# Values of two batches cast while loading on the GpSimd DMA queue, and a first batch that begins with 512 tokens

## Chip, core and metric

The kernel runs on one core of a Trainium2 chip. The metric is the device time of one execution in microseconds (us), lower is better. Every time below is a median of at least four runs, and each ratio is against runs of the kernel before on the same chip. The experiments were spread over three chips; the kernel before took 226.0 to 226.5 us in every set, so medians of different sets may be compared to about half a microsecond. A profile shows one execution; its span is some 1.7 us shorter than the time of the run it comes from.

Names: TensorE is the matrix engine (PE), VectorE is DVE, ScalarE is ACT, GpSimd is POOL, SyncE is SP. Loads are issued on two queues, that of SyncE (a plain copy) and that of GpSimd (whose loads in these kernels cast float32 to bfloat16 on the way). The profile counts the packets of both against the same sixteen DMA engines: 49.6% of the engines' span for GpSimd's queue and 40.4% for SyncE's in the kernel before.

## The reference

```python
# q, k, v: (4, 8, 768, 64) float32; n_sink 4, window 128; w_in (512, 2048), w_out (2048, 512)
scores = q @ k.T / 8
keep   = is_sink | ((rel >= 0) & (rel < 128))        # first 4 keys, and the last 128
a      = softmax(where(keep, scores, -1e9))
x      = (a @ v).transpose(0, 2, 1, 3).reshape(3072, 512)
out    = relu(x @ w_in) ** 2 @ w_out
```

## The kernel before

Every piece of work is an `op`. When the kernel is built, a planner walks through all ops with estimated durations and decides the order in which each engine gets its instructions. The program holds one list of instructions per engine in that order. TensorE's pieces carry these names in the profile: `pt` transposes of q and k, `ps` scores, `po` attention times v, `px` transposes of x, `pm` the first layer, `py` the second.

How loads are ordered:

```python
def dma_op(queue, name, run, us, behind=None, takes=(), yields=()):
    def go(e):
        ds = run(e)
        if behind is not None:
            for d in ds:
                after_dma(d, loaded[behind])      # a real wait on the chip
        loaded[name] = ds[-1]
    # ... cut ...
    o.yields += [ops[y] for y in yields]          # only the planner sees this

# in the planner, for a load on queue e:
queue[e] = max([queue.get(e, 0.0), end + DMA_START[e]] + moved) + o.dma
```

`behind` makes a load wait on the chip until another has landed. `yields` only tells the planner that a load will be late. The planner's `queue[e]` gives each queue a bandwidth of its own: it has no term for what the loads of one queue take from those of the other (measured below: 25 GB/s for q and k beside w_out, for 245 to 265 alone). The list of loads in the kernel before (its lines, some cut):

```python
for g, m0 in ((0, 0), (0, 2), (1, 0), (1, 2)):    # batch 0 in blocks of 256 tokens, two head pairs a load
    for ti in (1, 0):
        load_qk(0, m0, ti, g)
    if g:
        load_v(0, m0 // 2)                        # SyncE, float32; an engine casts it later
# ... cut ...
for i in range(4):
    load_w_in(i, ("qk", 0, 2, 1, 1) if i == 0 else None)              # GpSimd, cast
load_w_out(0)
load_w_out(1)
for m0 in (0, 2):
    for ti in (1, 0):
        load_qk(0, m0, ti, 2, ("w_out", 0) if m0 == 0 and ti == 1 else None, [("w_out", 1)])
load_v(0, 2, None, ())
load_w_out(2, ("v", 0, 4), [("v", 0, 5)])                             # wait (a)
load_w_out(3, None, ())
for m0 in (0, 2):
    for ti in (1, 0):
        load_qk(1, m0, ti, 0, ("w_out", 2) if m0 == 0 and ti == 1 else None, [("w_out", 3)])   # wait (b)
# ... cut: the rest of batch 1 ...
# batches 2 and 3 load q, k and v with a cast on GpSimd; the first one:
    ("v", 1, 3) if (b, ti, t) == (2, 1, 0) else None                  # wait (c)
```

I call the three marked waits (a), (b) and (c).

The softmax here doesn't subtract the row's maximum and nothing guards it: scores larger than these inputs give would overflow.

## Time and profile before

| | before |
|---|---|
| time, median of 4 in the rounds of the comparison | 226.51 us (226.32 to 226.72) |
| profiled span | 224.3 us |
| TensorE busy | 217.0 us, 97% |
| first layer matmul starts | 18.59 us |
| granted TensorE clock | full in all 40 slices |

The page's list of DMA issues (what, issuing queue, count, size of one, median us from issue to landing) of the kernel before:

```profile
vf<-in_v_dram SPq DMA_DIRECT2D x12, 256.0 KB, 5.4
qr<-in_k_dram SPq DMA_DIRECT2D x8, 256.0 KB, 4.8
qr<-in_q_dram SPq DMA_DIRECT2D x8, 256.0 KB, 4.5
w_in_sb<-in_moe_w_in_dram POOLq DMA_DIRECT2D x4, 512.0 KB, 8.3
w_out_sb<-in_moe_w_out_dram POOLq DMA_DIRECT2D x4, 512.0 KB, 9.3
```

### The profile page before, as it was taken

What the parts mean: (1) busy time and instruction counts of PE and PEld (TensorE: products, weight loads), DVE (VectorE), ACT (ScalarE), POOL (GpSimd) and SP (SyncE); (2) the same over time, 40 slices, a digit from 0 to 9 for tenths busy, and PEclk for the clock granted to TensorE, in tenths of its full rate; (3) what the DMA queues carried; (4) which work ended last, traced back from release to release, by engine and by line L of the source; (5) the groups of instructions that cost most, each with busy time, mean ns of one, the idle gap of its engine ahead of it and who ended that gap; (6) DMA issues with size and microseconds to landing.
All of it is one profiled execution on the core that took longest, in us unless ns stands there. A gap on an engine that the chain in (4) does not pass through costs nothing.

```text
span 224.3 us, 4593 instructions
## 1 busy us (share of the span) xinstructions
PE 217.0 (97%) x1941; PEld 137.5 (61%) x1941; DVE 103.9 (46%) x190; ACT 115.2 (51%) x130; POOL 62.7 (28%) x97
## 2 busy tenths in 40 slices
PE   7899999999999999999999999999999999999993
PEld 7557996457865796555454555587464555874441
DVE  7573535466775577446372533456344123440010
ACT  2387465517785587287636275675433066551010
POOL 5179015134389935977300000000002000000000
PEclk9999999999999999999999999999999999999999
DMA  5999986999999999999999552000121430000222
GB/s 162 263 202 207 215 218 150 186 337 288 192 260 145 125 202 131 165 137 202 154 130 151 144 155 55 3 0 17 33 105 28 128 117 3 0 0 3 93 95 94
DMA packets 86357, 29.70 MB, mean 132 GB/s; under 512 B 70336, under 2 KB 82880, under 8 KB 86336
## 3 DMA queue, kind: packets, MB, share of 16 engines
q0 software_dynamic: 40128, 8.92, 49.6%
q1 hardware_dynamic: 46024, 20.35, 40.4%
q8 instruction: 15, 0.25, 0.5%
q10 hardware_dynamic: 184, 0.14, 0.2%
q14 instruction: 6, 0.05, 0.1%
HBM read 27.30 MB, written 6.29 MB: 150 GB/s over the span
## 4 chain that ended last, share of the span: by engine, by line
PE 89%; ACT 4%; DMA 3%; DVE 1%; SPq 1%; issue 0%; ACTq 0%
PE pm L701 38%; PE py L741 37%; PE po L641 6%; PE ps L580 4%; DMA qr<-in_q_dram 3%; ACT r L710 2%; PE pt L477 1%; SPq L345 1%; ACT expm L599 1%; PE px L678 1%; DVE qkT L208 1%; ACT qkT L206 1%; PE pk L540 1%; PE ps L573 0%; DVE qs L208 0%
## 5 line engine op out<-in xcount | busy, mean ns | idle before, releaser
L741 PE MATMUL py<-w_out_sb,gT 128*128 128x512 bf16 x384 | 88.8, 379 | 0.0
L701 PE MATMUL pm<-xT,w_in_sb 128*128 128x256 bf16 (+1 forms) x576 | 87.0, 308 | 0.8 <-ACT r L710 0.6
L701 PEld LDWEIGHTS <-w_in_sb 128*128 128x128 bf16 x576 | 62.9, 114 | 21.5 <-issue 2.1
L710 ACT ACTIVATE r<-pm 128x1024 bf16<-128x1024 f32 x48 | 49.2, 1026 | 33.3 <-PE pm L701 26.8
L741 PEld LDWEIGHTS <-gT 128*128 128x128 bf16 x384 | 35.4, 98 | 38.5 <-issue 1.4
L599 ACT ACTIVATE expm<-ps 128x1024 bf16<-128x1024 f32 (+1 forms) x48 | 43.3, 953 | 22.6 <-PE ps L580 21.4
L717 DVE TENSOR_TENSOR gT<-r 128x1024 bf16<-128x1024 bf16 x48 | 33.6, 699 | 44.4 <-ACT r L710 44.3
L608 DVE TENSOR_TENSOR expm<-expm,mask 128x1024 bf16<-128x1024 bf16 (+1 forms) x37 | 24.7, 675 | 16.5 <-ACT expm L599 15.8
L206 ACT ACTIVATE osb<-py 128x1024 f32<-128x1024 f32 x10 | 10.3, 1027 | 24.9 <-PE py L741 17.8
L222 POOL TENSOR_SCALAR_AFFINE_SELECT expm<-expm 128x512 bf16<-128x512 bf16 x4 | 2.5, 637 | 66.4 <-ACT expm L599 62.1
L641 PEld LDWEIGHTS <-expm 128*128 128x128 bf16 x352 | 16.6, 97 | 4.9 <-issue 0.8
L641 PE MATMUL po<-v,expm 128*128 128x65 bf16 x352 | 17.9, 193 | 0.3 <-DVE v L208 0.2
L653 DVE TENSOR_TENSOR xn_sb<-po,rc 128x512 bf16<-128x512 f32 x24 | 16.6, 692 | 0.8
L652 DVE RECIPROCAL rc<-po 128x8 f32<-128x8 f32 x24 | 5.0, 207 | 24.2 <-PE po L641 23.9
L580 PE MATMUL ps<-qkT 64*128 64x128 bf16 (+1 forms) x256 | 14.7, 238 | 0.1
L580 PEld LDWEIGHTS <-qkT 64*128 64x128 bf16 x256 | 8.1, 94 | 10.3 <-issue 8.9
L641 PE MATMUL po<-vs,es 128*128 128x65 bf16 x128 | 13.1, 193 | 0.0
L210 POOL CAST qs<-qr 128x512 bf16<-128x512 f32 x11 | 7.1, 649 | 18.7 <-PE pm L701 10.1
L208 DVE COPY osb<-py 128x1024 f32<-128x1024 f32 (+2 forms) x3 | 2.3, 781 | 21.0 <-PE py L741 17.9
L388 POOL DMA_DIRECT2D v<-in_v_dram x12 | 10.6, 894 | 4.0 <-DMA qn<-in_q_dram 3.7
L641 PEld LDWEIGHTS <-es 128*128 128x128 bf16 x128 | 11.7, 97 | 0.0
L378 POOL DMA_DIRECT2D qn<-in_k_dram x12 | 10.8, 911 | 2.4 <-DMA vf<-in_v_dram 2.3
(51 smaller groups left out, 112.7 us busy)
## 6 DMA issues: line engine op xcount, KB each, us to landing
out_dram<-osb SPq DMA_DIRECT2D x11, 512.0 KB, 3.2
vf<-in_v_dram SPq DMA_DIRECT2D x12, 256.0 KB, 5.4
qr<-in_k_dram SPq DMA_DIRECT2D x8, 256.0 KB, 4.8
qr<-in_q_dram SPq DMA_DIRECT2D x8, 256.0 KB, 4.5
w_in_sb<-in_moe_w_in_dram POOLq DMA_DIRECT2D x4, 512.0 KB, 8.3
w_out_sb<-in_moe_w_out_dram POOLq DMA_DIRECT2D x4, 512.0 KB, 9.3
qn<-in_k_dram POOLq DMA_DIRECT2D x12, 128.0 KB, 8.0
qn<-in_q_dram POOLq DMA_DIRECT2D x12, 128.0 KB, 10.0
```

Source lines behind the costliest of these rows:

```text
L206: nc.scalar.activation(out=dst, in_=src, func=AF.Copy)
L378: return [nc.gpsimd.dma_start(out=qn_t[b, ti][:, t, :].rearrange("p (h d) -> p h d", d=D), in_=(q, k)[ti][b, :, 128 * t:128 * t + 128, :]. ...
L388: return [nc.gpsimd.dma_start(out=v_sb[b % 2][:, t, :, 0:D], in_=v[b, :, 128 * t:128 * t + 128, :].rearrange("h p d -> p h d"))]
L580: nc.tensor.matmul(ps[:, h2, o:o + w], lhsT=qkT_sb[r, m, 1, c, :], rhs=qkT_sb[r, m, 0, qb:qb + w // 128, :], start=(i == 0 and not biased) ...
L599: nc.scalar.activation(out=x[:, :, o:512], in_=bank_t["s", b, s, m][:, :, o:512], func=AF.Exp, scale=scale)
L608: nc.vector.tensor_mul(x[:, :, o:512], x[:, :, o:512], mk[:, :, o:512])
L641: nc.tensor.matmul(pv[:, i, h2, :], lhsT=lhsT, rhs=rhs, start=(n_ == 0), stop=(n_ == len(mms) - 1))
L653: nc.vector.tensor_tensor(out=xn_sb[:, 2 * s:2 * s + 2, 128 * m0:128 * m0 + 256].rearrange("p i (j h d) -> p j i h d", j=2, d=D), in0=pv[: ...
L701: nc.tensor.matmul(pm[:, i, :], lhsT=w_in_sb[:, fb // 4, kb, fb % 4:512:4], rhs=xT[:, c0 // 256:(c0 + cw) // 256, kb, :], start=(kb == 0), ...
L710: nc.scalar.activation(out=r, in_=bank_t.pop(tag), func=AF.Relu)
L717: (nc.vector if e == "dve" else nc.gpsimd).tensor_mul(gT_sb[c0 // 512][:, fbs[0]:fbs[0] + n, c0 % 512:c0 % 512 + cw], r, r)
L741: nc.tensor.matmul(pm[:, i, :], lhsT=gT_sb[t // 4][:, fb, 128 * (t % 4):128 * (t % 4) + 128], rhs=w_out_sb[:, fb, :], start=(fb == 0), sto ...
```

## The change

The intent: v of batches 0 and 1 is cast by its load on GpSimd's queue, as v of batches 2 and 3 is already, so six casts go. Batch 0 begins as one block of 512 tokens, with one head pair a load, so rows are 1024 B and not 512 B. The planner's numbers are tuned anew. The core of the diff, with cuts:

```diff
-    GROUPS[0] = [(0, 2), (256, 2), (512, 2)]
+    GROUPS[0] = [(0, 4), (512, 2)]
 # ... load_v:
-            dma_op("sp", ("v", b, t), run, 8 * 8 * ROW[256], behind if i == 0 else None,
-                   [sl] if i == 0 else (), yields)
+                return [nc.gpsimd.dma_start(
+                    out=v_sb[b % 2][:, t, :, 0:D],
+                    in_=v[b, :, 128 * t:128 * t + 128, :].rearrange("h p d -> p h d"))]
+            o = dma_op("pool", ("v", b, t), run, 1.15, behind if t == 2 * s else None, (), yields)
 # ... the casts of v go:
-                    copy(e, vb[:, 2 * s:2 * s + 2, :, 0:D], vf_t.pop((b, s)))
 # ... the casting loads of batch 2:
-                           ("v", 1, 3) if (b, ti, t) == (2, 1, 0) else None,
+                           None,
 # ... the list of loads:
+    load_v(0, 0, ("qk", 0, 1, 0, 0))
+    load_v(0, 1)
-            load_qk(0, m0, ti, 2, ("w_out", 0) if m0 == 0 and ti == 1 else None, [("w_out", 1)])
-    load_v(0, 2, None, ())
-    load_w_out(2, ("v", 0, 4), [("v", 0, 5)])
-    load_w_out(3, None, ())
+            load_qk(0, m0, ti, 1, 2, ("w_out", 0) if m0 == 0 and ti == 1 else None)
+    load_v(0, 2)
+    load_w_out(2)
+    load_w_out(3)
-            load_qk(1, m0, ti, 0, ("w_out", 2) if m0 == 0 and ti == 1 else None, [("w_out", 3)])
+            load_qk(1, m0, ti, 0, 2, ("v", 0, 5) if m0 == 0 and ti == 1 else None)
 # ... planner numbers, for example:
-PE_SLACK = 0.219
+PE_SLACK = 0.356
-    LO, HI = 0.03, 0.504
+    LO, HI = 0.12, 0.628
```

Once v is on GpSimd's queue, an old wait such as "w_out 2 behind v" would lie within one queue, so it was dropped. All three waits, (a), (b) and (c), are gone or weaker in the changed kernel, and so are the planner's `yields`.

## The prediction

> **What bounds the kernel now.** I read the page's busy shares first, then the chain of work that ended last, then the timeline of its head, then the costs of single forms.
>
> ```profile
> PE 217.0 (97%) x1941; PEld 137.5 (61%) x1941; DVE 103.9 (46%) x190; ACT 115.2 (51%) x130; POOL 62.7 (28%) x97
> PE 89%; ACT 4%; DMA 3%; DVE 1%; SPq 1%; issue 0%; ACTq 0%
> ```
>
> TensorE is the bound: 97% busy, 89% of the chain. So the change can matter in two ways only: it moves the time at which TensorE becomes dense, or it adds or removes holes after that. The chain in order of time (start, length, what) shows both:
>
> ```profile
> 3.61 5.69 DMA qr<-in_q_dram
> 12.71 2.33 ACT expm L599 x3
> 18.59 1.94 PE pm L701 x16
> 24.18 10.48 PE pm L701 x96
> 58.66 1.03 ACT r L710
> 61.68 1.03 ACT r L710
> 81.27 1.03 ACT r L710
> 84.29 1.03 ACT r L710
> 199.92 20.73 PE py L741 x96
> 220.68 0.39 ACT half L206
> ```
>
> Until 18.59 us the chain passes through loads, casts, copies and exponentials of batch 0; there the first layer matmul starts. From then on it is TensorE, except four waits for a ReLU of ScalarE. Around each wait the next 16 pm matmuls start 1.07 to 1.15 us after the last ended (58.58 to 59.73, for one): 4.4 us of holes. From 220.68 on there is a tail of 3.6 us that the change does not touch.
>
> I checked this with a sum of TensorE's own work, at the rates of the chain's full pieces: py and 512-wide pm 20.73/96 = 0.216 us, 256-wide pm 0.108, po 0.73/24 = 0.030, transposes 0.45/8 = 0.056, score pieces 0.44 for 8 and 0.55 for 12. Counts times rates: py 82.9, pm 82.9, po 14.5, scores with bias 15.1, transposes of q, k and x 8.0, sink scores 1.5; together 205 us, warm-up matmuls left out. Of it 8.1 lies before 18.59. The remaining 196.8 take 220.7 - 18.6 = 202.1, so 5.3 us are lost after the head: the 4.4 above and 0.9 in crumbs.
>
> [...] in the packet records, 512 B packets took 27 to 29 ns on the SyncE queue and moved 245 to 265 GB/s in the first microseconds; 1024 B packets (batch 1's loads, 46 to 50 us) took 47 to 49 ns and moved about 350 GB/s. [...] In this trace the cast loads of v for batches 2 and 3 cost GpSimd 894 ns each to issue, and 2400 of their packets went through in 2 us (66 to 70 us), so a load of 1024 packets takes about 0.85 us of the engines; whether such a load starves one on the SyncE queue, no run here shows yet. [...]
>
> **The change, part by part.** I compared the order of instructions per engine of the two programs.
>
> *TensorE's work is the same* apart from 74 warm-up matmuls for 61, all in the head's gaps. So there is no gain from less work. What moves: before, the first layer matmuls on tokens 0 to 255 came at 18.59, in front of the second half's values and transpose of x. Now all values (48 more matmuls, 1.45 us) and 8 more transposes of x (0.45 us) come first, and then 128 pm matmuls without a break. If the first pm starts at T, break-even is T = 18.6 + 1.9 = 20.5.
>
> *Casts of v.* Gone are six: four on VectorE at 0.69 and two on GpSimd at 1.05, 4.9 us in all, none of it in the dense part's chain. GpSimd gets 12 issues of about 0.9, 10.7 us; it was 28% busy. In the head VectorE loses two casts of v and the four sink-value products (1.18 us, 4.07 to 5.25), which held up the first cast of k: that load had landed at 3.9 and was cast at 5.28.
>
> *Loads of q and k.* Eight of 256 KB either way. Before, landings were at 3.9, 4.7, 6.4, 7.5, 8.4, 9.3, and behind two loads of v 12.4 and 13.4. With 1024 B rows (0.75 us a load in place of 0.93 to 0.95) and v out of their queue I estimate 3.7, 4.4, 5.5, 6.3, 7.0, 7.6, 8.3 and 9.0. VectorE and ScalarE then cast as they land.
>
> *The head's new limit is ScalarE.* In the new order it stands so: copy, cast of the third k, copy, cast of the fourth k, then eight exponentials, one copy, the sinks' exponential, two copies of x. The cast of the fourth k cannot start before its landing at 8.3 and takes about 0.6 (a 128x512 copy there takes 0.60), so exponentials start at 8.9. Four of 128x768 and four of 128x1024 with the copy and the sinks, at the back-to-back steps seen before (0.83, 0.97, 0.6, 0.39), are 3.3 + 3.9 + 0.6 + 0.4 = 8.2: the last ends at 17.1 if four PSUM banks let TensorE stay ahead, which they do in my walk through the order (a bank freed by an exponential is refilled within 0.8 us). Then the last values (0.73), the transposes of the first x, which stand behind them (0.45), and ScalarE's copy of it (1.02), with 0.15 to 0.2 between steps: 17.1 + 0.2 + 0.75 + 0.45 + 0.15 + 1.02 + 0.2 = 19.9. T = 19.9, and the head gains 20.5 - 19.9 = 0.6 us.
>
> *Weights.* The first w_in was issued at 12.73 and landed at 18.5. Now it follows four issues of v, which start when the fourth load has landed (6.3): issue at about 10, landing about 16. Not the limit. The later ones are 2.5 us apart and needed every 3.5.
>
> *The holes later.* The pair at 58 to 62 came from pm blocks alternating with pairs of q/k transposes, so that ScalarE did a ReLU (1.03) and two copies (1.2) in each 1.75 us of pm. In the new order these pm blocks stand apart, with layer-2 matmuls, values or scores between, and batch 1's loads come earlier, behind v of batch 0 (landing near 31 us) rather than the third w_out. I expect no full pair there, but 0.5 us in crumbs as TensorE waits for PSUM banks of transposes and sinks. The pair at 81 to 84 came where ScalarE had about 10.9 us of ReLUs, exponentials and copies against 8.6 of TensorE. The new order has a like stretch (two score groups of batch 1, two of batch 2, four pm blocks): 11.4 against 9.5, and the banks held in hand cover part, so 0.8 stays. With 0.4 for a late q/k load of batch 0's last 256 tokens I put 1.7 in place of 4.4: gain 2.7.
>
> Sum: 0.6 + 2.7 = 3.3 us. 226.67 - 3.3 = 223.4, or 1.5% less.
>
> **The rivals.** *Loads collide.* The cast loads of v, then w_in and w_out, run beside the SyncE loads without the old order among them. For it: each load of w_out now shares engines with batch 1's q and k, and packets of 4096 B take 324 ns against 47. Against: batch 0's last transposes have about 1 us and batch 1's several us of slack in my estimate. If the SyncE loads stand still behind every w_out, one hole of 1 to 2 us opens near 34 us: 224.5 to 225.5. *ScalarE's head is longer.* If a bank is not free in time at each of the eight exponentials, or v lands late, 1.5 us are added: T = 21.4, time 225. For it: scores and values share four banks. *The holes stay*, because ScalarE's work is the same and only moved: then only the head counts: 226. *No holes at all and a head at 19.3*: another 2.3 off, 221.1; for it: ScalarE is only 51% busy and the order was plainly tuned anew (the planner's constants changed).
>
> **Range and chances.** The head's error I put at 1 us either way, the holes' at 1.5; together somewhat under 2, wider upward because of the collisions: 221.5 to 225.8. Faster by over 2% means under 222.1, which needs both errors in the good direction: 0.19. Slower by over 2% needs 7.8 us of new waits, and nothing I see is that large: 0.02. Within 2%: 0.79.
>
> **What would show it.** In the changed profile: the first pm near 19.9, with ScalarE nearly unbroken from 9 to 17; the first k cast on VectorE before 4.5; q and k all landed by 9.5; v's casts gone; and between the first pm and 200 us fewer than two chain pieces of a full ReLU. I am wrong if pm starts after 20.5, if the chain has DMA or casts in it near 34 us, or if the ReLU waits are as many as before.

## The result, and the profile after

| | before | after |
|---|---|---|
| time, median of 4 | 226.51 us | 238.13 us (237.04 to 239.20) |
| ratio | | 1.0512, 95% interval 1.046 to 1.0565 |
| profiled span | 224.3 us | 235.3 us |
| first layer matmul | 18.59 us | 22.10 us |

A ratio is the mean time of one kernel's fast runs over that of the other's of the same rounds, so it is not quite the ratio of the medians quoted. The changed kernel is 5.1% slower. The prediction of 223.4 us, and its range up to 225.8, are wrong.

The page of the changed kernel, busy time, granted clock in tenths per slice of the span, and shares of the chain that ended last:

```profile
PE 218.6 (93%) x1935; PEld 138.9 (59%) x1954; DVE 101.1 (43%) x188; ACT 118.2 (50%) x135; POOL 66.5 (28%) x98
...
PEclk9999999799999999999999999999999999999999
...
PE 72%; DMA 16%; POOL 6%; issue 1%; DVE 1%; ACT 1%; SPq 1%; POOLq 0%
```

TensorE does no more work than before, but DMA is now 16% of the chain, for 3%. One slice of the clock is a 7. The same chain in order of time (start, length, what):

```profile
2.45 4.43 DMA qr<-in_q_dram
7.50 3.90 POOL v L361 x4
11.40 2.91 POOL w_in_sb L300 x4
14.32 14.52 DMA w_out_sb<-in_moe_w_out_dram
29.34 11.45 DMA qr<-in_q_dram
...
50.32 7.86 DMA qr<-in_q_dram
...
96.29 1.03 ACT r L703
```

The chain now runs through loads until 41 us: through the first w_out, which releases batch 0's last loads of q and k, and through one of those, which needs 11.45 us. It comes back to a load of q at 50 us. The ReLU waits, four before, are one. Where TensorE stood idle (us in all, times, longest):

```profile
PE pt L476 <- POOL qs L210: 6.5, 3, 3.8
...
PE po L634 <- DMA v<-in_v_dram: 1.2, 1, 1.2
PE pt L476 <- DVE qs L208: 1.0, 1, 1.0
```

The releaser named, the cast of q and k to `qs`, had itself waited for its load. The busy time per stretch of the kernel before, and then of the changed one, says when:

```profile
core 0: us, PE busy (x) PEld busy (x) DVE busy (x) ACT busy (x) POOL busy (x), PEclk, DMA share, GB/s
36.00:45.00 9.00, 8.90 (x93) 4.69 (x92) 4.47 (x6) 5.03 (x7) 3.11 (x5) 1.00 0.83 157
45.00:66.00 21.00, 20.38 (x209) 15.13 (x206) 14.68 (x27) 13.26 (x18) 10.29 (x15) 1.00 1.05 279
```

```profile
36.00:45.00 9.00, 4.00 (x21) 1.96 (x20) 2.49 (x4) 1.62 (x2) 2.66 (x4) 0.81 1.40 224
45.00:66.00 21.00, 17.78 (x203) 10.91 (x204) 14.42 (x27) 12.93 (x19) 14.76 (x19) 1.00 1.72 219
```

In the first stretch TensorE works 4.00 of 9 us and is granted 0.81 of its clock; in the second it lacks another 2.6 us. And the list of DMA issues of the changed kernel, against the one shown of before:

```profile
v<-in_v_dram POOLq DMA_DIRECT2D x24, 128.0 KB, 9.8
qr<-in_k_dram SPq DMA_DIRECT2D x8, 256.0 KB, 9.2
qr<-in_q_dram SPq DMA_DIRECT2D x8, 256.0 KB, 8.9
...
w_out_sb<-in_moe_w_out_dram POOLq DMA_DIRECT2D x4, 512.0 KB, 16.4
```

Loads of q and k take twice as long from issue to landing, and w_out nearly twice.

**Where the 11 us went.** By the sum of TensorE's own work used in the prediction, break-even for the first `pm` was 20.5 us. It came at 22.10, so the head costs 1.6 us. TensorE then has 194.9 us of work left (204.9 by the counts and rates of the prediction, less the 10.0 done by then) and ends at 231.4: it loses 14.4 us there, for 5.3 before. Together 1.6 + 9.1 = 10.7 us. I count from known counts and rates, as 17 of the 384 `py` records are missing from this trace. Of the 14.4 us, 4.8 are two idle stretches between 36.23 and 41.29 us, before the transposes of batch 0's last 256 tokens. About 1.5 are the half clock after them: TensorE was busy for 3.5 of the 4 us from 41 to 45, at a granted 0.50 until 44.4. (Weight loads of `py` came 0.43 us apart there, from 42.33 to 44.04, where a `py` takes 0.216 us at full clock.) And 3.1 are idle stretches between 54.9 and 64.2 us, before transposes of batch 1. The other 5.0 us are crumbs, about what the kernel before lost in all (5.3).

**Why the loads are late.** The packet records of the changed kernel between 33 and 36 us, when w_out (rows of 4096 B) and batch 0's last q and k (rows of 512 B) were both under way, by queue: packets, MB, and time taken as a share of 16 engines:

```profile
q0 software_dynamic: 152, 0.56, 91.9%
q1 hardware_dynamic: 150, 0.08, 12.2%
```

q0 is GpSimd's queue and q1 SyncE's. In 3 us the two get the same number of packets, 152 and 150. That is fair by packets, but a packet of w_out took 324 ns and one of q or k about 40. So SyncE's loads moved 0.08 MB in 3 us, about 25 GB/s, where such rows moved 245 to 265 GB/s alone in the first microseconds of the kernel before. At 38 to 42 us the other queue carries v in packets of 128 B, and the counts are again 1314 against 1457; SyncE then gets about 165 GB/s. Equal or nearly equal counts stand too at 46 to 50 us (980 and 980) and in the stretches of e5, e8 and e12 below. Three of the four loads of q and k for batch 0's last 256 tokens landed at 40.8 us or later, after TensorE had run dry at 36.2.

The packet records do not name the DMA engine. They show the counts of the two queues, and not how an engine chooses between them.

**The theory and its rivals.** Theory: the three dropped waits let loads of the two queues meet, the SyncE loads get a small share, and TensorE runs dry. Rival 1: v on the GpSimd queue itself costs the time, because issues there occupy GpSimd (0.89 us for each load of v of batches 2 and 3 in the kernel before) and its casts are slower (1.05 us for a cast of v, for 0.69 on VectorE). Rival 2: the long packets of w_out alone are at fault. Rival 3: the new planner numbers, or the start of 512 tokens, cost it with no collision at all.

### The profile page after: what moved, and what is told of

Same layout as the page of the kernel before. It is cut to its first block, busy times and chain, and to the rows that moved or that the text cites. A ratio compares the mean times of both kernels' runs of the same rounds, so it can differ in the third digit from the quotient of the medians.

```text
span 235.3 us, 4596 instructions
## 1 busy us (share of the span) xinstructions
PE 218.6 (93%) x1935; PEld 138.9 (59%) x1954; DVE 101.1 (43%) x188; ACT 118.2 (50%) x135; POOL 66.5 (28%) x98
## 4 chain that ended last, share of the span: by engine, by line
PE 72%; DMA 16%; POOL 6%; issue 1%; DVE 1%; ACT 1%; SPq 1%; POOLq 0%
PE py L734 33%; PE pm L694 29%; DMA qr<-in_q_dram 10%; DMA w_out_sb<-in_moe_w_out_dram 6%; PE po L634 5%; PE ps L571 4%; POOL qn L380 2%; POOL v L361 2%; POOL w_in_sb L300 1%; POOL qs L210 1%; PE pt L476 1%; SPq L348 1%; POOL v L390 1%; DVE qs L208 1%; PE pk L531 0%
## 5 line engine op out<-in xcount | busy, mean ns | idle before, releaser
L734 PE MATMUL py<-w_out_sb,gT 128*128 128x512 bf16 x367 | 86.8, 383 | 1.3 <-issue 0.5
L694 PEld LDWEIGHTS <-w_in_sb 128*128 128x128 bf16 x576 | 62.8, 114 | 20.2 <-issue 1.6
L734 PEld LDWEIGHTS <-gT 128*128 128x128 bf16 x384 | 36.0, 99 | 40.7 <-issue 3.2
L599 DVE TENSOR_TENSOR expm<-expm,mask 128x1024 bf16<-128x1024 bf16 (+1 forms) x39 | 26.2, 674 | 28.2 <-ACT expm L590 27.5
L206 ACT ACTIVATE osb<-py 128x1024 f32<-128x1024 f32 x11 | 11.3, 1024 | 36.3 <-PE py L734 36.2
L476 PE MATMUL pt<-ident,qs 128*128 128x128 bf16 x96 | 8.3, 233 | 8.1 <-POOL qs L210 6.5
L206 ACT ACTIVATE qkT<-pt 128x512 bf16<-128x512 bf16 x14 | 7.8, 596 | 15.9 <-DVE qkT L208 8.2
L476 PEld LDWEIGHTS <-qs 128*128 128x128 bf16 x96 | 6.3, 105 | 10.1 <-POOL qs L210 7.2
L208 DVE CAST qs<-qr 128x512 bf16<-128x512 f32 x12 | 6.3, 527 | 12.5 <-DMA qr<-in_q_dram 10.9
L380 POOL DMA_DIRECT2D qn<-in_q_dram x12 | 10.7, 897 | 3.6 <-DMA qn<-in_k_dram 3.3
```

The lines of the kernel that those rows point to most:

```text
L206: nc.scalar.activation(out=dst, in_=src, func=AF.Copy)
L476: nc.tensor.matmul(pt[:, j if w == 2 else ti, o + 128 * t:o + 128 * t + 128], lhsT=qs[ti][:, j, t, :, :], rhs=ident, is_transpose=True, st ...
L599: nc.vector.tensor_mul(x[:, :, o:512], x[:, :, o:512], mk[:, :, o:512])
L694: nc.tensor.matmul(pm[:, i, :], lhsT=w_in_sb[:, fb // 4, kb, fb % 4:512:4], rhs=xT[:, c0 // 256:(c0 + cw) // 256, kb, :], start=(kb == 0), ...
L734: nc.tensor.matmul(pm[:, i, :], lhsT=gT_sb[t // 4][:, fb, 128 * (t % 4):128 * (t % 4) + 128], rhs=w_out_sb[:, fb, :], start=(fb == 0), sto ...
```

## The experiments

All outputs were correct except in one run, which is marked.

### 1. One wait at a time

**e3_before_ungated**: the kernel before, with wait (a) alone removed.

```diff
-    load_w_out(2, ("v", 0, 4), [("v", 0, 5)])
+    load_w_out(2, None, ())
```

> The kernel before, only the wait of the third w_out load dropped (v stays on SyncE with a cast on an engine). Theory A: a hole of 3 to 7 us opens before batch 0's last transposes near 36 us and the time rises to 230 to 236. Theory B: no hole, the time stays within 1% of the kernel before.

Measured: 229.62 us, ratio 1.015 (1.0133 to 1.0167). A hole opens at the place where the changed kernel has its largest one, 36.50 to 38.96 us, and a second of 0.48. The waits of TensorE, first line:

```profile
PE pt L477 <- POOL qs L210: 3.3, 3, 2.5
```

One dropped wait, with nothing else of the change, makes 1.5% and the first hole of the changed kernel, at some six tenths of its size (2.46 and 0.48 us, for 3.78 and 1.00). What follows the hole is as instructive. The granted clock (second number from the end but one: busy times, then PEclk, DMA share, GB/s), in steps of 1 us:

```profile
37.00:38.00 1.00, 0.00 (x0) 0.00 (x0) 0.00 (x0) 0.00 (x0) 0.00 (x0) 1.00 1.16 333
38.00:39.00 1.00, 0.04 (x1) 0.04 (x2) 0.00 (x0) 0.00 (x0) 0.61 (x1) 0.87 1.19 287
39.00:40.00 1.00, 0.52 (x4) 0.25 (x5) 0.00 (x0) 0.00 (x0) 0.61 (x1) 0.50 1.25 230
...
44.00:45.00 1.00, 1.00 (x4) 0.34 (x3) 0.65 (x2) 0.83 (x1) 0.56 (x2) 0.50 1.07 373
```

The hole of 2.5 us is followed by 6.6 us at half the clock (until 45.6): four `py` matmuls took 1.71 us at 40.66, and 0.86 at 51.24. In this run the loss at the hole is more than its length.

**e12_before_batch2_free**: the kernel before, with wait (c) alone removed.

```diff
-                           ("v", 1, 3) if (b, ti, t) == (2, 1, 0) else None,
+                           None,
```

> The kernel before, only the wait of batch 2's casting loads for batch 1's v dropped, as the change drops it. Theory A: batch 2's loads start near 45 us in place of 62.4, run beside batch 1's q, k and v on SyncE, these land later by 3 us or more, and TensorE waits for the last transposes of batch 1 between 50 and 65 us: 228 to 233. Rival: that wait has no part in it: within 0.5% of the kernel before.

Measured: 242.64 us, ratio 1.0729 (1.07 to 1.0758). Batch 2's casting loads now run beside batch 1's loads of v on SyncE. The packet records from 58 to 66 us:

```profile
q0 software_dynamic: 5162, 0.65, 126.6%
q1 hardware_dynamic: 2590, 0.65, 58.6%
...
vf<-in_v_dram SPq DMA_DIRECT2D x3, 256.0 KB, 10.7
```

A load of v takes 10.7 us here, for a median of 5.4 in the kernel before. (The counts over the whole stretch are not equal, because SyncE had little under way from 59 to 61 us (104 packets against 2280); from 64 to 65 us, when both had work, they are 414 and 413.) TensorE waits once for 5.74 us, at 69.87 to 75.60 us, before `po` of batch 1: the last load of v landed at 73.68, and its cast and a mask followed. So (c), not (a), is the dearest of these waits when it is taken away alone. But not all of the 7.3% lies there: TensorE also stands for 4.8 us after 100 us, where scores and values wait for exponentials and a transpose of x in an order laid anew. That the collision led to this is not shown.

**e1_wout2_gated**: the changed kernel, with the like of (a) put back.

```diff
-    load_w_out(2)
+    load_w_out(2, ("qk", 0, 2, 0, 1))
```

> The changed kernel, only the third w_out load waits again for the last q load of batch 0 (v stays on the GpSimd queue). Theory A, the SyncE loads of q and k for batch 0's last 256 tokens are starved by the unbroken stream of casting loads (w_out 1 to 3 and v), because the change dropped that wait: these loads land by about 36 us in place of 39.2 to 43.9, the TensorE hole before the transposes (4.8 us at 36 to 41) shrinks below 1.5 us, and the time falls to 229 to 234. Theory B, it is v on the GpSimd queue in itself that starves or delays them: the hole stays above 3 us and the time stays above 236.

Measured: 239.97 us, ratio 1.0596: no gain. The hole before batch 0's last transposes did go. What came in its place, by TensorE's waits:

```profile
PE py L734 <- DMA w_out_sb<-in_moe_w_out_dram: 2.7, 1, 2.7
PE pt L476 <- DVE qs L208: 2.0, 3, 1.5
```

TensorE now waits for w_out itself (42.24 to 44.97 us), as w_out 2 and 3 land later beside batch 1's loads. A single wait put back moved the collision, and did not remove it.

**e13_batch2_waits**: the changed kernel, with the like of (c) put back.

```diff
-                           None,
+                           ("qk", 1, 2, 0, 1) if (b, ti, t) == (2, 1, 0) else None,
```

> The changed kernel, only batch 2's casting loads wait for batch 1's last q load. Theory A: the second hole (2.1 us at 56.8 to 59.0 and 0.6 at 63.5) goes or shrinks below 1 us, the first one at 36 to 41 stays: 233 to 237. Rival: nothing moves.

Measured: 243.90 us, ratio 1.0803: worse. The first hole stays (5.07 and 0.83 us from 34.8 us), the second shrinks from 3.1 to 2.1 us, and new ones of 2.9 us appear near 141 to 146 us, where scores of late batches wait for exponentials. Alone it does not help. The likely reason, not tested, is that batches 2 and 3 now begin later in an order that was not made for it.

**e1b_gated_b1_behind**: the changed kernel, with the like of (a) and (b).

```diff
-    load_w_out(2)
+    load_w_out(2, ("qk", 0, 2, 0, 1))
-            load_qk(1, m0, ti, 0, 2, ("v", 0, 5) if m0 == 0 and ti == 1 else None)
+            load_qk(1, m0, ti, 0, 2, ("w_out", 2) if m0 == 0 and ti == 1 else None, [("w_out", 3)])
```

> The changed kernel with both waits of the kernel before put back: w_out 2 behind batch 0's last q load, batch 1's q and k behind w_out 2. If the two dropped waits are the whole of the loss after the head: no hole above 1.5 us between 30 and 50 us, time 227 to 230, the rest being the head (first layer matmul at 21.5 to 22). If v on the GpSimd queue is what costs (v of batch 1 and batch 2's casting loads stand in the way of batch 1's q and k): holes near 50 to 65 us stay, time above 233.

Measured: the result was wrong (relative error 0.48). I don't know why, and draw nothing from its 240.16 us.

### 2. Is it GpSimd, the planner's ignorance, or the packet size?

**e5_v_on_sync**: the changed kernel, with v loaded by SyncE again and cast by an engine, but the waits still dropped.

```diff
-                return [nc.gpsimd.dma_start(
-                    out=v_sb[b % 2][:, t, :, 0:D],
+                return [nc.sync.dma_start(
+                    out=vf_t[b, s][:, i], in_=v[b, :, 128 * t:128 * t + 128, :].rearrange("h p d -> p h d"))]
```

> The changed kernel with v of batches 0 and 1 put back on SyncE with a cast on an engine; 512-token start and the dropped wait of w_out kept. Theory A: the hole near 36 us stays (3 us or more) and the time is 233 or more. Theory B: the hole goes and the time is under 230. For the head: if the late v [...] is what put the first layer matmul at 22.1, it now comes before 21.5; if not, it stays at 22 or later.

Measured: 240.30 us, ratio 1.0642. (Not shown: the wait of v for a load of q goes too, as both are now in one queue.) Taking v off the GpSimd queue does not help while nothing keeps the queues apart. But the hole that the theory expected near 36 us did not stay: TensorE was busy for 29.84 of the 30 us from 30 to 60. It stood for 7.09 us at 16.94 to 24.03 instead, before `po`, waiting for v. Loads of w_in, in casting packets of 1024 B, now meet v in packets of 256 B, with equal counts again (about 150 to 160 of each per us), and v gets 40 GB/s. The first `pm` slips to 27.94 us. So a collision can do this without v on the GpSimd queue. Rival 1 in its plain form, that v there costs the time in itself, is tested better by e15 below, where v stays there and 1.7% is left.

**e4_plan_told**: the changed kernel, with the planner told that batch 0's last q and k will be late. The waits on the chip are the same.

```diff
-            load_qk(0, m0, ti, 1, 2, ("w_out", 0) if m0 == 0 and ti == 1 else None)
+            load_qk(0, m0, ti, 1, 2, ("w_out", 0) if m0 == 0 and ti == 1 else None, [("w_out", 3)])
```

(The lines also move behind the w_out loads in the list.)

> The changed kernel with the same waits in hardware, only the planner is told that the q and k loads of batch 0's last tokens yield to w_out 3, so it puts 32 layer-2 matmuls (6.9 us) in front of the transposes. Theory A with the loss being TensorE's idle time: the loads still land near 39 to 44 us, but the hole is filled, and the time falls to 229 to 233. Rival C, w_out itself is what comes late: the layer-2 matmuls wait for w_out instead and the time stays above 235.

Measured: 239.60 us, ratio 1.0598. The planner put 32 `py` matmuls first, and the hole at 36 us is filled. But TensorE then waits 4.17 us at 57.20 to 61.37 us, before `px`. The late load is still late: its work was only put off.

**e7_last_loads_early**: the changed kernel, with batch 0's last q and k released by v and no longer by w_out 0.

```diff
-            load_qk(0, m0, ti, 1, 2, ("w_out", 0) if m0 == 0 and ti == 1 else None)
+            load_qk(0, m0, ti, 1, 2, ("v", 0, 3) if m0 == 0 and ti == 1 else None, [("w_in", 3)])
```

(The planner is also told that batch 1's loads come after w_out 3.)

> The changed kernel, q and k of batch 0's last tokens released by v 3 in place of w_out 0, so that they share the engines with w_in (packets of 98 ns), and the planner told that batch 1's q and k come after w_out 3. Theory A: they land by 28 us, no hole at 36 to 41 us; batch 1's loads still run beside w_out, so some loss near 45 to 60 remains: 228 to 234. Rival: w_in becomes late instead and layer 1 waits before 36 us, time above 236.

Measured: 241.83 us, ratio 1.071. The loads now meet w_in and w_out 0 instead, and the holes are 2.51 us at 30.7, 1.54 at 36.6, and 2.95 and 1.02 at 57.8 to 62.1. To start earlier beside the other queue is no way out.

**e8_short_w_out**: the changed kernel, with w_out laid out in packets of 1024 B instead of 4096. TensorE's order is the same, instruction for instruction.

```diff
-                in_=moe_w_out[512 * i:512 * i + 512, :].rearrange("(p f) m -> p f m", p=128))],
+                in_=moe_w_out[512 * i:512 * i + 512, :].rearrange("(f p) m -> p f m", p=128))],
```

(w_in's columns are read in the matching order.)

> The changed kernel, only the rows of w_out are laid so that its casting load writes packets of 1024 B (about 98 ns each) in place of 4096 B (324 ns); TensorE's order of instructions is the same to the last matmul. Theory A[...]: a 512 B SyncE packet now waits 98 ns and not 324, so beside w_out the SyncE queue moves about 80 GB/s in place of 25, the loads of q and k for batch 0's last tokens land by 37 to 40 us in place of 39.2 to 43.9, the TensorE hole at 36 to 41 shrinks from 4.8 to under 2.5 us, and the time falls by 2 to 5 us, to 233 to 236. Rival: the share is by bytes or the delay is in the issue; then nothing moves (237 to 239).

Measured: 238.31 us, ratio 1.0529: the same as the change. Packets per queue at 35 to 37 us:

```profile
q0 software_dynamic: 327, 0.29, 86.8%
q1 hardware_dynamic: 287, 0.15, 36.1%
```

This is the cleanest test of the sharing. Packets are still about one for one, so with shorter ones on the other queue SyncE gets 0.15 MB in 2 us, some 74 GB/s instead of 25. But w_out 0, which releases those loads, now landed at 30.59 us, for 28.84 in the changed kernel, and in three of the four loads one of the sixteen parts came 0.7 to 1.7 us after the others. So the first landed 0.5 us earlier (38.67), the others 1.4 to 2.4 us later, and the holes are 3.78 and 2.77 us. The size of w_out's packets sets SyncE's share; what that share is worth in time this run cannot say. Rival 2, that the long packets alone are at fault, falls by e12, where the loss arises beside packets of 128 B.

### 3. v alone, and the queues kept apart

**e6_before_v_pool**: the kernel before, with v on GpSimd's queue and nothing else of the change; (a) is kept in a like form, (c) is dropped.

```diff
-                return [nc.sync.dma_start(
-                    out=vf_t[b, s][:, i], in_=v[b, :, 128 * t:128 * t + 128, :].rearrange("h p d -> p h d"))]
+                return [nc.gpsimd.dma_start(
+                    out=v_sb[b % 2][:, t, :, 0:D],
+                    in_=v[b, :, 128 * t:128 * t + 128, :].rearrange("h p d -> p h d"))]
-    load_w_out(2, ("v", 0, 4), [("v", 0, 5)])
+    load_w_out(2, ("qk", 0, 2, 0, 2))
```

> The kernel before with v of batches 0 and 1 cast while loading on the GpSimd queue, nothing else of the change: 256-token start, waits of w_out 2 and of batch 1's q and k kept. Theory A: little lost where the waits keep the queues apart, 225 to 229. Theory B (v on the GpSimd queue in itself): 232 or more.

Measured: 241.32 us, ratio 1.0648. With (c) dropped, which alone cost 7.3% in e12, this does not show what v by itself costs.

**e11_before_v_pool_apart**: the same, with v of batch 0's last block and of batch 1 held behind SyncE's loads. w_out 2 follows v in its queue.

```diff
-    load_v(0, 2, None, ())
-    load_w_out(2, ("v", 0, 4), [("v", 0, 5)])
+    load_v(0, 2, ("qk", 0, 2, 0, 2), ())
+    load_w_out(2, None)
-    load_v(1, 0, None, ())
+    load_v(1, 0, ("qk", 1, 2, 0, 1), ())
```

> The kernel before with v cast while loading on the GpSimd queue, but kept apart from q and k in the same way. Theory A: 225 to 230, against 239 to 243 of the same kernel without the waits. Theory B: it stays above 234.

Measured: 235.73 us, ratio 1.0408. Keeping the queues apart gives back 5.6 us of the 15, less than the theory said (225 to 230 us).

**e10_kept_apart**: the changed kernel, with its GpSimd loads kept apart from SyncE's q and k.

```diff
-    load_v(0, 2)
+    load_v(0, 2, ("qk", 0, 2, 0, 1))
-            load_qk(1, m0, ti, 0, 2, ("v", 0, 5) if m0 == 0 and ti == 1 else None)
-    load_v(1, 0)
-    load_v(1, 1)
+            load_qk(1, m0, ti, 0, 2, ("w_out", 2) if m0 == 0 and ti == 1 else None, [("w_out", 3)])
 # ... after batch 1's last q and k:
+    load_v(1, 0, ("qk", 1, 2, 0, 1))
+    load_v(1, 1)
```

> The changed kernel with every GpSimd load kept apart from the SyncE loads of q and k: v of batch 0's last tokens behind its last q load, w_out 2 and 3 after that, batch 1's q and k behind w_out 2, v of batch 1 (and with it, on the same queue, batch 2's loads) behind batch 1's last q load. Theory A [...]: no hole above 1.5 us between 30 and 66 us, granted clock 0.99 or more, time 226 to 230, what is left being the head. Theory B (GpSimd's work for v in itself, or the 512-token start in itself): 233 or more.

Measured: 233.45 us, ratio 1.0314 (1.029 to 1.0338), 4.7 us less than the changed kernel. Its DMA issues:

```profile
qr<-in_k_dram SPq DMA_DIRECT2D x8, 256.0 KB, 5.4
qr<-in_q_dram SPq DMA_DIRECT2D x8, 256.0 KB, 5.2
...
w_out_sb<-in_moe_w_out_dram POOLq DMA_DIRECT2D x4, 512.0 KB, 11.6
```

Loads of q and k are back near the 4.5 to 4.8 us of before, no hole is longer than 1.4 us, and the granted clock is 0.992 to 1.000 in its runs (0.971 to 0.993 in those of the changed kernel). These were the theory's signs, and so the meeting of the queues is a cause. But the time is the one for the rival (233 or more): seven of the 11.6 us were left.

### 4. What the other seven microseconds are

**e14_before_new_numbers**: the kernel before, with only the planner numbers of the change.

```diff
-PE_SLACK = 0.219
+PE_SLACK = 0.356
-    LO, HI = 0.03, 0.504
+    LO, HI = 0.12, 0.628
 # ... and the margins and start times, as in the change
```

> The kernel before with nothing of the change but its planner numbers (the start of each batch, the margins, the slack, the stretch keys); loads, casts and all three waits as before. Theory (the two DMA queues meeting is the main cause, the numbers are only tuned to it): 226 to 229 us. Rival (the new order of the schedule is itself what costs the 7 us left with the queues kept apart): 231 us or more, with holes on TensorE whose releasers are not loads.

Measured: 229.03 us, ratio 1.0119 (1.0087 to 1.0151). Its idle stretches are few: one of 1.00 us at 76.2 (`px` waits for VectorE) and others under 0.7. That is at the upper edge of the outcome that the theory gave.

**e16_512_start_alone**: the kernel before, with only the start of 512 tokens; v stays on SyncE, all waits and numbers of the kernel before.

```diff
-    GROUPS[0] = [(0, 2), (256, 2), (512, 2)]
+    GROUPS[0] = [(0, 4), (512, 2)]
```

> The start of batch 0 as 512 tokens, one head pair a load, alone: v on the SyncE queue with its casts, all three waits and the planner numbers of the kernel before. If this part is harmless, as my prediction had it: 225 to 229 us, first pm at 19 to 22 us. If it is a main part of the loss: 231 us or more, with first pm after 24 us or holes before 45 us.

Measured: 232.89 us, ratio 1.0298 (1.0266 to 1.0331). In time this is the second outcome, but its signs are not: no hole lies before 45 us. Its first `pm` came at 21.01 us, on the wrong side of break-even. The rest is neither in the head nor at the old holes: some 3.9 us of idle time lie between 130 and 137 us, where scores wait for exponentials, and the clock is halved for 3.4 us. TensorE's order there is a new one. So "harmless" is refuted, though most of the cost is what the new order did 110 us later.

**e15_apart_old_numbers**: e10, with the planner numbers of the kernel before.

```diff
-PE_SLACK = 0.356
+PE_SLACK = 0.219
-    LO, HI = 0.12, 0.628
+    LO, HI = 0.03, 0.504
 # ... and the margins and start times, as in the kernel before
```

> The changed kernel with its queues kept apart (as e10, 233.45 us) and with the planner numbers of the kernel before. If the numbers are most of what is left there: 227 to 230 us. If v on the GpSimd queue or the start of 512 tokens is: 232 to 236 us, with holes before po (waiting for v) or before py (waiting for w_out).

Measured: 230.10 us, ratio 1.0168 (1.0119 to 1.0216). First `pm` at 20.63, at break-even; its landings:

```profile
qr<-in_k_dram SPq DMA_DIRECT2D x8, 256.0 KB, 4.8
qr<-in_q_dram SPq DMA_DIRECT2D x8, 256.0 KB, 4.7
```

These are before's. What is left are idle stretches of 0.98 us at 51.7 and 1.11 us at 59.8, at the end of chains through batch 1's q and k, which stand behind w_out 2; and w_out 2 stands behind v in the GpSimd queue.

**e17_change_old_numbers**: the changed kernel as it is, with the planner numbers of the kernel before; the same lines as e15, on the changed kernel.

```diff
-PE_SLACK = 0.356
+PE_SLACK = 0.219
 # ... and the other numbers, as in the kernel before
```

> The changed kernel as it is, with its dropped waits and its collisions, and only the planner numbers of the kernel before. With the changed kernel (238.13 us), with the queues kept apart (233.45) and with both (230.10) it makes a square of four. If the meeting of the queues costs about the same under either set of numbers: 234 to 236 us. If the collisions matter only under the new numbers: 229 to 232 us. If the old numbers do nothing while the queues meet: 237 to 240 us. Holes before pt near 36 us and near 57 us are expected in the first and the third case.

Measured: 242.44 us, ratio 1.0696 (1.0639 to 1.0752): above every outcome. I had not thought that the old numbers could make the changed kernel worse. Its chain at the place in question:

```profile
13.74 15.78 DMA w_out_sb<-in_moe_w_out_dram
31.08 13.52 DMA qr<-in_q_dram
```

TensorE idles for 4.30, 1.21 and 0.69 us between 36 and 45.5 us, and the granted clock is 0.83 from 36 to 66 us. With this run the square is complete (medians, ratios against before):

| | queues meet | queues kept apart | difference |
|---|---|---|---|
| the change's numbers | 238.13 us, 1.0512 (the change) | 233.45 us, 1.0314 (e10) | 4.7 us |
| the old numbers | 242.44 us, 1.0696 (e17) | 230.10 us, 1.0168 (e15) | 12.3 us |

The totals differ, 12.3 us under the old numbers and 4.7 under the change's. But they hold more than the collisions. Busy time by stretch, of e10, then of e15, then of e17:

```profile
36.00:66.00 30.00, 26.93 (x261) 17.53 (x260) 13.73 (x27) 14.70 (x20) 15.56 (x23) 1.00 0.96 197
```

```profile
36.00:66.00 30.00, 26.83 (x274) 17.66 (x275) 16.46 (x32) 17.00 (x23) 14.86 (x20) 1.00 1.00 198
100.00:150.00 50.00, 49.74 (x374) 27.17 (x376) 22.14 (x37) 28.51 (x31) 11.92 (x15) 1.00 1.17 125
```

```profile
36.00:66.00 30.00, 23.54 (x203) 13.72 (x206) 15.17 (x30) 11.14 (x15) 15.00 (x19) 0.83 1.92 207
100.00:150.00 50.00, 46.50 (x371) 24.43 (x375) 22.91 (x40) 26.84 (x31) 14.77 (x18) 0.93 1.29 126
```

From 36 to 66 us, where q and k meet the other queue, I add TensorE's idle time and half of the work that it did at half clock. The changed kernel loses 9.7 us there (8.2 and 1.5), e10 loses 3.1: 6.6 us for the meeting. e17 loses 9.9 (6.5 and 3.4), e15 3.2: 6.7 us. So where the queues meet, the meeting costs about the same under both sets of numbers (from one profile of each). The rest of the 12.3 us is that e17 loses 6.3 us from 100 to 150 us, for 0.3 in e15, where scores wait for exponentials as in e16. The rest of the small 4.7 us is mostly that e10 loses 3.8 us from 66 to 150 us, for 0.7 in the changed kernel. Both are orders that the planner laid anew; why it laid these is open. Rival 3 holds in part: the numbers and the new start have a cost of their own, of 1 to 3% (e14, e16), and 3.4 us with the queues apart. The collision is the largest single term.

No version beat the kernel before; the nearest were e14 (1.0119), e3 (1.015) and e15 (1.0168).

**What stays open.** Every edit but e8 makes the planner lay out TensorE's work anew, so the single costs do not add: (c) alone cost 7.3%, and v with (c) dropped 6.5%, more than the whole change. No run changed the waits with TensorE's order held. The ratios say that each piece, taken alone, hurts a schedule tuned around it; they are not shares of the 5.1%. By time, most forecasts of the theory failed: e1, e4, e6, e7, e8, e10 and e11 fell in the range for a rival, e12 and e13 lay above any. What carries it is the packet counts, the landings and the idle stretches, not the times. How much of e15's 1.7% is v in the GpSimd queue and how much the start of 512 tokens is not settled.

## Why the prediction was wrong

- *TensorE's work is the same.* Right: 217.0 and 218.6 us busy, and the excess includes pieces at half clock.
- *Loads of q and k, "With 1024 B rows (0.75 us a load in place of 0.93 to 0.95)".* Wrong in size. They landed at 3.53, 4.71, 6.16, 6.88, 7.98, 8.72, 9.44 and 10.17 us: 0.95 us a load on average. The last three steps were the forecast 0.72 to 0.74 us; the first were up to 1.45. From 2 to 6 us packets of 1024 B took 57 to 58 ns on average, and moved 273 GB/s. I had taken 47 to 49 ns and 350 GB/s from another stage of the trace.
- *"exponentials start at 8.9", "T = 19.9".* Exponentials started at 10.06, and the second half of the first v landed at 14.90 us because one of its sixteen parts came 2.1 us after the others. TensorE stood for 1.17 us before `po`. T was 22.10, past the break-even of 20.5, so the gain of 0.6 us became a loss of 1.6. The rival "or v lands late" had named this wait. In nine other runs that share this head T lay between 20.2 and 21.7 us: this is partly scatter, but at best (20.23, e17) a gain of 0.3 us.
- *"The holes later" and their gain of 2.7 us.* Wrong, and from a misread line. The ReLU waits did fall from four pieces of the chain to one. But the "4.4 us of holes" were for the most part not idle time: the chain follows one block of `pm` through its ReLU to the next, and TensorE worked on other pieces meanwhile. After the block that ended at 58.40, 16 transposes ran, started 0.056 us apart, the last at 59.24; the next `pm` came at 59.73. TensorE was idle for about 0.44 us, and for 0.41, 0.26 and 0.28 at the other three waits, 1.4 us in all. The list of waits of the kernel before counts two of them, after the ends of the matmuls:

```profile
PE pm L701 <- ACT r L710: 0.6, 2, 0.3
```

  So 2.7 us were not there to be gained, and no gain shows in the sum: the crumbs after the change (5.0 us) are as large as the whole loss before (5.3).
- *"With 0.4 for a late q/k load of batch 0's last 256 tokens".* This is the term that failed most. It measured 4.8 us of idle time, about 1.5 of half clock behind it, and 3.1 more at batch 1's loads: 9.4 us in place of 0.4.
- *The rival "Loads collide".* It named the cause, the packets of 4096 B at 324 ns against 47, and the place, "near 34 us" for a measured 36. Its size, "one hole of 1 to 2 us", was wrong because I reasoned that "batch 0's last transposes have about 1 us and batch 1's several us of slack". With equal packet counts (152 and 150) the SyncE rate near w_out was 25 GB/s: an estimate of 1 MB of q and k (four loads of 256 KB) at that rate is 40 us, so no slack of a few us could cover it. I had both packet times before me and did not divide them.
- *"whether such a load starves one on the SyncE queue, no run here shows yet".* It does, twice: q and k beside w_out (the changed kernel, 25 GB/s for 245 to 265 alone), and v beside batch 2's casts (e12, 10.7 us a load for 5.4).
- *"Slower by over 2% needs 7.8 us of new waits, and nothing I see is that large: 0.02".* The waits dropped from the list were in the diff, three of them. I read them as bookkeeping of the move to another queue, and not as what kept two queues from meeting. e3 and e12 show 1.5% and 7.3% for two of them, each dropped alone.
- *The tests it set itself.* "I am wrong if pm starts after 20.5, if the chain has DMA or casts in it near 34 us": both happened, and q and k landed by 10.17 and not 9.5. The third, as many ReLU waits as before, did not.

## What to carry to other kernels

When a change moves a load to another DMA queue, list the waits that disappear with it, and ask of each what it kept apart on the chip, not only which data it guarded. In these traces two queues that had work at once got nearly equal numbers of packets (152 and 150, 1314 and 1457, 327 and 287), so divide the packet times of what will run together to get the bandwidth that the urgent load keeps (for e8 this gave an estimate of about 80 GB/s; 74 were measured). A piece of the chain is a path of waits and not idle time: look at what the engine did meanwhile before counting it as a hole. And when a planner lays the work anew at each edit, compare losses by stage; the totals here showed 4.7 and 12.3 us for what cost 6.6 and 6.7 where it happened.

## What the traces show and do not explain

All of this was measured in the profiles of this case.

- Packet counts were 152 against 150 from 33 to 36 us of the changed kernel (4096 B against 512 B), and the SyncE queue moved about 25 GB/s, for 245 to 265 alone in the first microseconds of the kernel before. With 1024 B on the other queue it got 74 (e8, 35 to 37 us), with 128 B about 165 (the changed kernel, 38 to 42 us). How a DMA engine chooses between the queues no run shows.
- The same 1024 B packets of the same queue took 57 to 58 ns on average from 2 to 6 us of the changed kernel, 47 to 49 ns from 6 us on, and 47 to 49 ns at 46 to 50 us in the kernel before. What makes the difference no run shows.
- In e3 the granted clock halved some 2.2 us into a hole of 2.46 us and stayed at 0.50 for 6.8; in e16 it halved at 135.4 us, when no hole of the ten microseconds before was longer than 1.5 us. In the changed kernel it halved at 41.0 us, 4.8 us after the hole began, and stayed at 0.50 for 3.4, and holes of up to 1.4 us left it at 1.000 in e10. What decides it no run shows.
- A load leaves sixteen landing records. One of them came 2.1 us after the other fifteen for v (14.90 us for 12.78 at the latest of the rest, in the changed kernel), and 3.1 and 3.0 us for the third and fourth load of w_out in e8. In e8 one landing of some SyncE loads lagged too, by up to 1.7 us. The records do not say which DMA engine it was.
